# A fused adaLN, linear attention and GEGLU kernel: first-LN transposes by DMA, den and broadcasts by pairs of token groups, woven among Q blocks and KV*wo

## The chip, the cores, the metric

One NeuronCore of one Trainium2 chip. The metric is the device time of one execution in microseconds, and smaller is better. A quoted time is the median of a kernel's runs in the fast state. A profile describes one of those executions; its span is about 1.8 us shorter than that execution's time (899.0 us beside 900.79 for the kernel before).

Engines, as the profile names them: PE is TensorE (PEld its weight loads), DVE is VectorE, ACT is ScalarE, POOL is GpSimd, SP is SyncE, which issues most DMAs. In the traces each engine takes its instructions in the order of the program: VectorE's scaling at 287.46 us below, for instance, stands behind two modulations that it does not need. The granted clock is the share of full speed that TensorE's clock was given, as the profile records it; a stretch near 0.5 is called cold.

## The reference, cut to what matters

```python
# x: 2048 tokens x 1024, bf16; 32 heads of 32; F = 3584
h = _layernorm(x) * (1 + ca) + sa             # first LN, modulated by a row per feature
q, k, v = split(h @ wqkv)
phi = lambda t: where(t > 0, t + 1, exp(t)) + 1e-6
kv = einsum('bhsd,bhse->bhde', phi(k), v)     # over ALL tokens
z  = einsum('bhsd->bhd', phi(k))
den = einsum('bhqd,bhd->bhq', phi(q), z) + 1e-6
x = x + ga * ((phi(q) @ kv / den) @ wo)
h = _layernorm(x) * (1 + cb) + sb             # second LN
x = x + gb * ((gelu(h @ w_gate) * (h @ w_up)) @ w_down)
```

kv and z need every token before the first output of the attention can be made. So the program has a first pass over 16 chunks of 128 tokens (LN, K, V, accumulation of kv, and Q of earlier token groups beside it), then an end of that pass with the last Q group and den, then the output product, then the FFN over four groups of 512 tokens.

## The kernel before

`T, A, V, G, Q` are TensorE, ScalarE, VectorE, GpSimd and SyncE. `sch.op` appends an instruction to an engine's list and works out its waits from the bytes that it reads and writes, so the order of these Python lines is the order of each engine's work. Cuts are marked `# ...`.

```python
def t1(c_, tb):            # transpose chunk c_ of the normalised x into h1T
    for dc in range(NDC):
        sch.op(T, lambda e, dc=dc: e.transpose(PS16(tb, dc * P, (dc + 1) * P), b_[:, dc * P:(dc + 1) * P], IDENT[:, :]), ...)
    sch.op(A, lambda e: e.activation(H1[sg][:, :, ci * P:(ci + 1) * P], PS16(tb)..., ACTF.Copy), ...)

def phi(bank, dst_ap, dst_rng, note):      # exponential, min/add, addition
    sch.op(A, ... e.activation(EB[i], PS(bank), ACTF.Exp) ...)
    sch.op(V, ... e.tensor_scalar(EB[i], EB[i], 1.0, 1e-6, op0=ALU.min, op1=ALU.add) ...)
    sch.op(V, ... e.scalar_tensor_tensor(dst_ap, PS(bank), 0.0, EB[i], op0=ALU.max, op1=ALU.add) ...)

for c_ in range(4, NCH):                        # THE LOOP
    # ...
    if c_ + 2 < NCH:
        t1(c_ + 2, 4)                           # PSUM bank 4
        if c_ % 2 == 1:
            mod1(c_ + 1, 2)                     # x(1+ca)+sa of two chunks, on VectorE
    for _ in range(2):
        q_block(*q_todo.pop(0))
    # ... two K blocks, two V blocks, each with its eviction
    kvacc(c_ - 1)
    if c_ + 3 < NCH:
        ln1(c_ + 3)                             # statistics and normalisation of chunk c_+3, on VectorE
    # ... at 6 and 9: modulation rows through bank 4; at 10: selector matrices on GpSimd

q_block(3, 0)                                   # THE LAST Q GROUP
kvacc(NCH - 1)
q_block(3, 1)
zcols()
kvbd()
q_block(3, 2)
den(0)                                          # 32 matmuls 128 wide, reciprocal, split in two bf16
kvt()
q_block(3, 3)
for g in range(NG):
    w2_pair(g)                                  # KV*wo: two matmuls, a copy of 128x1024 by ScalarE
    if g % 2 == 1:
        q_block(3, 4 + g // 2)
    if g == 3:
        den(1)
den(2)
# ... bcast(0, 0..1): spread 1/den over the features in PSUM; pq_scale: multiply phi(q) by it

for sg in range(3):                             # THE WO STAGE, chunks 0 to 11
    for ci in range(CPG):
        c_ = sg * CPG + ci
        wo_chunk(c_, 4 + 2 * (ci % 2))          # 16 matmuls, then x1 = PSUM + x on VectorE
        if ci < 2:
            bcast(sg + 1, ci)
            for j in range(CPG):
                pq_scale(sg + 1, ci, j)
        if c_ == 2:
            den(3)
        if sg == 1:
            ln2_a(ci, False)                    # second LN of chunk ci, its DMA transpose
            if ci == 3:
                mod2(0, 2)
    if sg == 1:
        mod2(2, 2)                              # waits for the transposes of chunks 2 and 3
# ... FFN; wo chunks 12 to 15 stand in it
```

Of the kernel before, what the change touches and what calls it, by code (L numbers as in the profile page):

```python
# [10 lines left out]
P = 128  # L11
# [205 lines left out]
def bass_adaLN_cond__linear_attn_block__geglu_ffn__prompt_kernel(  # L217
# [14 lines left out]
    with ExitStack() as es:  # L232
# [30 lines left out]
        RDHL = at("rdhl", [P, NSG, 2, P], bf16, OFF_RDHL)  # L263
# [24 lines left out]
        for name, shape, dty, sz in [  # L288
            ("ident", [P, P], bf16, 256), ("bmask", [P, P], bf16, 256), ("bm32", [P, NG, NH], bf16, 512),
            ("z32", [P, NG, NH], bf16, 512), ("rd0", [P, P], f32, 512), ("rd1", [P, P], f32, 512),  # L290
# [14 lines left out]
        RDC = [_small["rd0"], _small["rd1"]]  # L305
# [48 lines left out]
        def r_rdhl(sg, k):  # L354
            return [(OFF_RDHL + (sg * 2 + k) * 256, OFF_RDHL + (sg * 2 + k + 1) * 256, "rdhl")]
# [157 lines left out]

        def mods(Ht, rfn, sg, scT, biT, sn, bn, s0, s1, dc0=0, dc1=NDC, tag=""):
# [48 lines left out]
        def phi(bank, dst_ap, dst_rng, note):  # L563
# [4 lines left out]
            sch.op(V, lambda e: e.tensor_scalar(EB[i][:, :], EB[i][:, :], 1.0, 1e-6, op0=ALU.min, op1=ALU.add),  # L568
                   rd=rng, wr=rng, note=f"{note}.min")
# [45 lines left out]
        def q_block(sg, qc):  # L615
            b = nb()
# [7 lines left out]
            phi(b, PQ[sg][:, qc, :], r_pq(sg, qc, qc + 1), f"phiq{sg}.{qc}")  # L624
# [32 lines left out]
        for c_ in range(4):  # L657
            for jg in range(2):
                b = nb()
                kv_mm(c_, "v", jg, b, list(range(NDC)))  # L660
                v_evac(c_, jg, b)
            if c_ == 0:
                ln1(4)
                for k, t in enumerate((4, 5, 10, 11)):
                    wm_dma(t, k)
            if c_ >= 1:
                kvacc(c_ - 1)
            if c_ == 1:
                ln1(5)
            if c_ == 2:  # L670
                t1(4, 4)
                mod1(4, 1)
                ln1(6)
                x_dma(12, 16)
        t1(5, 4)
        mod1(5, 1)
# [3 lines left out]
        for c_ in range(4, NCH):  # L680
            if c_ % 4 == 0:
                q_todo += [(c_ // 4 - 1, qc) for qc in range(NG)]
            if c_ + 2 < NCH:
                t1(c_ + 2, 4)
                if c_ % 2 == 1:
                    mod1(c_ + 1, 2)
# [6 lines left out]
            for jg in range(2):  # L693
                b = nb()
                kv_mm(c_, "v", jg, b, list(range(NDC)))
                v_evac(c_, jg, b)
            kvacc(c_ - 1)
            if c_ + 3 < NCH:
                ln1(c_ + 3)
            if c_ == 6:  # L700
# [16 lines left out]
            if c_ == 10:  # L717
# [37 lines left out]
        def w2_pair(g):  # L755
            b0 = 4 + 2 * (g % 2)
# [7 lines left out]
        def den(sg):  # L764
            b = nb()
            o = None
            for g in range(NG):
                for j in range(CPG):
                    o = sch.op(T, lambda e, g=g, j=j: e.matmul(ps_all[32 * j:32 * (j + 1), b * 512:b * 512 + P], Z32[:, g, :],
                                                               PQ[sg][:, g, j * P:(j + 1) * P], start=(g == 0), stop=(g == NG - 1)),  # L770
                               rd=r_sm("z32") + r_pq(sg, g, g + 1, j * P, (j + 1) * P), pwr=(pr(b) if g == 0 else ()), note=f"den{sg} {g}.{j}")
            pset_writer(b, o)
            k = sg % 2
            rn = f"rd{k}"
            sch.op(V, lambda e: e.tensor_scalar(RDC[k][:, :], PS(b, 0, P), 1e-6, None, op0=ALU.add), prd=pr(b), wr=r_sm(rn), note=f"dene{sg}")
            sch.op(V, lambda e: e.reciprocal(RDC[k][:, :], RDC[k][:, :]), rd=r_sm(rn), wr=r_sm(rn), note=f"rden{sg}")
            sch.op(G, lambda e: e.tensor_copy(RDHL[:, sg, 0, :], RDC[k][:, :]), rd=r_sm(rn), wr=r_rdhl(sg, 0), note=f"rdhi{sg}")
            sch.op(G, lambda e: e.tensor_tensor(RDHL[:, sg, 1, :], RDC[k][:, :], RDHL[:, sg, 0, :], ALU.subtract),
                   rd=r_sm(rn) + r_rdhl(sg, 0), wr=r_rdhl(sg, 1), note=f"rdlo{sg}")

        def bcast(sg, gh):
            o = [None] * 4
            for g in range(4 * gh, 4 * gh + 4):
                for k in range(2):
                    for j in range(CPG):
                        b = j
                        o[j] = sch.op(T, lambda e, g=g, k=k, j=j, b=b: e.matmul(  # L787
                            PS(b, (g % 4) * P, (g % 4 + 1) * P), SEL[32 * j:32 * (j + 1), g, :], RDHL[32 * j:32 * (j + 1), sg, k, :],
                            start=(k == 0), stop=(k == 1)),
                            rd=R_SEL + r_rdhl(sg, k), pwr=(pr(b) if g % 4 == 0 and k == 0 else ()), note=f"bc{sg} {g}.{k}.{j}")  # L790
            for j in range(CPG):
                pset_writer(j, o[j])

        def pq_scale(sg, gh, j):
            ap = PQ[sg][:, 4 * gh:4 * gh + 4, j * P:(j + 1) * P]
            rng = r_pq(sg, 4 * gh, 4 * gh + 4, j * P, (j + 1) * P)
            sch.op(V, lambda e: e.tensor_tensor(ap, ap, PS(j).rearrange("p (a b) -> p a b", a=4), ALU.mult),
                   prd=pr(j), rd=rng, wr=rng, note=f"pqs{sg}.{gh}.{j}")

        q_block(3, 0)  # L800
        kvacc(NCH - 1)
        q_block(3, 1)
        zcols()
        kvbd()
        q_block(3, 2)
        den(0)
        kvt()
        q_block(3, 3)
        for g in range(NG):
            w2_pair(g)  # L810
            if g % 2 == 1:
                q_block(3, 4 + g // 2)
            if g == 3:
                den(1)
        den(2)
# [221 lines left out]
```

## Time and profile before

| | before |
|---|---|
| time, median of the first 3 runs (of 4 with the forecast's rounds) | 899.84 us (900.04) |
| span of the profiled run | 899.0 us |
| TensorE, first V block to first Q block | 40.62 to 58.95: 18.3 us |
| the loop, chunks 4 to 15 | 58.95 to 210.53: 151.6 us |
| last Q group, den, KV*wo, first broadcasts | 210.53 to 238.16: 27.6 us |
| wo stage, chunks 0 to 11 | 238.16 to 299.49: 61.3 us |
| FFN | 299.49 to the end: 599.5 us |

The stages are read from the timeline of TensorE, from the first matmul of one kind to the first of the next. Single matmul records can be missing from a trace, so an edge can be off by some 0.2 us.

Three lines of the page of the kernel before: busy time (us, share of the span, number of instructions), then TensorE's busy tenths and its granted clock in 40 slices of 22.5 us.

```profile
PE 852.5 (95%) x4569; PEld 394.2 (44%) x4569; DVE 503.4 (56%) x912; ACT 300.6 (33%) x481; POOL 36.2 (4%) x65
...
PE   3999998899895999999999999999999999999998
...
PEclk9999999999898999999999999999999999999999
```

TensorE is 95% busy. That does not say that nothing can be gained: the busy time of the page counts a matmul at a lower clock as fully busy (between 292 and 296 us below: 4.00 of 4.00 us busy at a clock of 0.71). The timeline says more. Its columns: start, duration, engine, line, operation, operands, number of instructions merged into the row, and in brackets the idle time before it and what ended it.

```profile
58.95 3.62 PE L619 MATMUL ps_all<-h1T_50,wq 128*128 128x512 bf16 x16
62.41 3.62 PE L578 MATMUL ps_all<-wk,h1T_51 128*128 128x512 bf16 x16
65.86 3.62 PE L578 MATMUL ps_all<-wv,h1T_51 128*128 128x512 bf16 x16
69.31 0.62 PE L600 MATMUL ps_all<-vs_78,pk_76 128*128 128x129 bf16 x8
70.93 0.62 PE L509 MATMUL ps_all<-ident,xh_105 128*128 128x128 bf16 x8 [1.00 <-DVE xh_105 L484]
71.39 3.62 PE L619 MATMUL ps_all<-h1T_50,wq 128*128 128x512 bf16 x16
```

Sixteen 128x512 matmuls take 3.45 us from start to start, 0.216 us each. One iteration needs 10.82 us of them: Q, K, V at 3.45 each and 0.45 for the accumulation (`vs,pk`). But the row at 70.93, the eight transposes of one chunk (`ident,xh`), is late by 1.00 us: it waited for VectorE's normalised chunk (`xh`). Such a wait, of 0.87 to 2.38 us, stands before the transposes of all iterations that have them (in two, 0.87 us each, it ends with ScalarE's copy of a modulation row). The longest such wait is this:

```profile
160.52 0.62 PE L600 MATMUL ps_all<-vs_79,pk_73 128*128 128x129 bf16 x8
163.51 0.62 PE L509 MATMUL ps_all<-ident,xh_106 128*128 128x128 bf16 x8 [2.38 <-DVE xh_106 L484]
163.97 5.30 PE L619 MATMUL ps_all<-h1T_52,wq 128*128 128x512 bf16 x16
```

After the wait of 2.38 us, sixteen Q matmuls take 5.14 us from start to start (163.97 to 169.11) instead of 3.45: the granted clock is 0.57 between 164 and 168.

The wo stage has the greatest loss. Rows 277.66 and 290.95 are output products (`w,pq`), those between them broadcasts (`rdhl,sel`):

```profile
277.66 3.63 PE L834 MATMUL ps_all<-w_65,pq_56 128*128 128x512 bf16 x16
288.19 0.28 PE L787 MATMUL ps_all<-rdhl,sel 32*128 32x128 bf16 x1 [6.91 <-DVE pq_57 L797]
288.79 0.28 PE L787 MATMUL ps_all<-rdhl,sel 32*128 32x128 bf16 x1 [0.32 <-DVE pq_57 L797]
...
290.95 8.71 PE L834 MATMUL ps_all<-w_65,pq_56 128*128 128x512 bf16 x32
```

TensorE stood for 6.91 us before one broadcast. It waited for VectorE's scaling L797. The same stretch on VectorE:

```profile
279.74 2.14 DVE L516 TENSOR_SCALAR h2T_58<-h2T_58,cb1T,sbT 128x256 bf16<-128x256 bf16 x8
284.27 2.14 DVE L516 TENSOR_SCALAR h2T_58<-h2T_58,cb1T,sbT 128x256 bf16<-128x256 bf16 x8 [2.39 <-DMA h2T_58<-xh_104]
286.33 1.22 DVE L841 TENSOR_TENSOR xall<-ps_all,xall 128x1024 bf16<-128x1024 f32 x1
287.46 2.47 DVE L797 TENSOR_TENSOR pq_57<-pq_57,ps_all 128x512 bf16<-128x512 bf16 x4
```

The row at 284.27, a second-LN modulation (L516), waited 2.39 us for a DMA transpose. The x1 additions (L841) and the scalings (L797), which TensorE needs, stand behind both modulations in VectorE's order although they do not depend on them. And windows of 4 us show what TensorE's standing costs afterwards (columns: window, length, busy time of the engines, the granted clock `PEclk`, DMA share, GB/s):

```profile
284.00:288.00 4.00, 0.00 (x0) 0.00 (x0) 3.73 (x10) 0.00 (x0) 0.00 (x0) 0.51 0.00 0
288.00:292.00 4.00, 2.86 (x35) 1.49 (x36) 4.00 (x7) 0.00 (x0) 0.00 (x0) 0.50 0.00 0
292.00:296.00 4.00, 4.00 (x14) 1.51 (x13) 1.46 (x3) 0.00 (x0) 0.00 (x0) 0.71 0.96 259
```

The granted clock is 0.51 and 0.50 in the first two of these windows and 0.71 in the third, and 32 matmuls from 291.01 on took 8.64 us in the chain of waits and not 6.91.

### The profile page before, as it was taken

To read this page: it belongs to the slowest core of one execution; us is meant where nothing else is said; L and a number is where in the kernel's file an instruction comes from. 1 tells how busy PE (TensorE), PEld (TensorE's weight loads), DVE (VectorE), ACT (ScalarE), POOL (GpSimd) and SP (SyncE) were. 2 spreads that over 40 slices of the span, in tenths; PEclk is the share of its full clock that TensorE was granted. 3 is DMA by queue.
4 is the path that set the end of the run, shared out by engine and by line. 5 is a ranking of instruction groups with operands and counts; after the bars stand their busy time and mean duration, and the time that the engine had idled before them with its cause. 6 is when DMAs were issued, how large, how long until landed. Compare 5 with 4: busy or idle time off the path is not lost.

```text
span 899.0 us, 11946 instructions
## 1 busy us (share of the span) xinstructions
PE 852.5 (95%) x4569; PEld 394.2 (44%) x4569; DVE 503.4 (56%) x912; ACT 300.6 (33%) x481; POOL 36.2 (4%) x65
## 2 busy tenths in 40 slices
PE   3999998899895999999999999999999999999998
PEld 2444444444342444444444444444444444444443
DVE  5476565666677455556436566535565643565512
ACT  4243333334201233453025454204545302545300
POOL 2000004200000000000000000000000000000000
PEclk9999999999898999999999999999999999999999
DMA  9940603000602345834135553306553413565000
GB/s 321 360 162 1 208 28 95 1 1 24 211 9 41 95 116 166 279 96 127 47 106 144 165 160 94 71 24 172 156 141 101 122 47 105 150 168 152 1 24 23
DMA packets 165096, 101.46 MB, mean 113 GB/s; under 512 B 21928, under 2 KB 157096, under 8 KB 165040
## 3 DMA queue, kind: packets, MB, share of 16 engines
q1 hardware_dynamic: 165040, 100.70, 38.9%
q8 instruction: 36, 0.59, 0.3%
q14 instruction: 20, 0.16, 0.1%
HBM read 92.28 MB, written 4.21 MB: 107 GB/s over the span
## 4 chain that ended last, share of the span: by engine, by line
PE 89%; DVE 6%; issue 2%; POOL 1%; ACT 1%; DMA 1%; SPq 0%; ACTq 0%; POOLq 0%; DVEq 0%
PE ps_all L897 22%; PE ps_all L921 22%; PE ps_all L894 21%; PE ps_all L578 10%; PE ps_all L619 6%; PE ps_all L834 5%; POOL rs L475 1%; DVE st L471 1%; PE ps_all L509 1%; DVE st L470 1%; PE ps_all L550 0%; PE ps_all L600 0%; PE ps_all L787 0%; PE ps_all L534 0%; PE ps_all L759 0%
## 5 line engine op out<-in xcount | busy, mean ns | idle before, releaser
L905 ACT ACTIVATE q_0_109<-ps_all 128x512 f32<-128x512 f32 x56 | 33.5, 598 | 183.3 <-PE ps_all L894 183.3
L927 DVE TENSOR_TENSOR ps_all<-ps_all,gbb 128x512 f32<-128x512 f32 x32 | 22.4, 698 | 95.7 <-PE ps_all L921 95.7
L907 DVE SCALAR_TENSOR_TENSOR ww_111<-q_0_109,ps_all 128x512 f32<-128x512 f32 x56 | 38.5, 687 | 56.9 <-ACT guh_96 L906 56.9
L910 DVE SCALAR_TENSOR_TENSOR ww_111<-th_113,guh_96 128x512 f32<-128x512 f32 x56 | 38.8, 693 | 39.0 <-ACT th_113 L909 39.0
L910 DVE SCALAR_TENSOR_TENSOR ww_112<-th_114,guh_97 128x512 f32<-128x512 f32 x56 | 38.8, 692 | 39.0 <-ACT th_114 L909 39.0
L907 DVE SCALAR_TENSOR_TENSOR ww_112<-q_1_110,ps_all 128x512 f32<-128x512 f32 x56 | 38.5, 687 | 37.1 <-ACT guh_97 L906 37.1
L905 ACT ACTIVATE q_1_110<-ps_all 128x512 f32<-128x512 f32 x56 | 33.5, 597 | 55.4 <-PE ps_all L894 54.2
L909 ACT ACTIVATE th_114<-ww_112 128x512 f32<-128x512 f32 x56 | 35.3, 630 | 42.2 <-DVE ww_112 L907 42.2
L909 ACT ACTIVATE th_113<-ww_111 128x512 f32<-128x512 f32 x56 | 35.3, 630 | 42.2 <-DVE ww_111 L907 42.2
L475 POOL TENSOR_TENSOR rs<-ve,neghalf 128x1 f32<-128x1 f32 x32 | 17.6, 551 | 606.3 <-DVE ve L473 592.7
L912 DVE TENSOR_TENSOR yT<-ww_111,ps_all 128x512 bf16<-128x512 f32 x56 | 38.4, 687 | 1.9
L912 DVE TENSOR_TENSOR yT<-ww_112,ps_all 128x512 bf16<-128x512 f32 x56 | 38.4, 687 | 1.9
L906 ACT ACTIVATE guh_96<-ps_all 128x512 f32<-128x512 f32 x56 | 33.1, 592 | 0.0
L906 ACT ACTIVATE guh_97<-ps_all 128x512 f32<-128x512 f32 x56 | 33.1, 592 | 0.0
L921 PE MATMUL ps_all<-wd_66,yT 128*128 128x512 bf16 x128 | 32.9, 379 | 0.0
L921 PE MATMUL ps_all<-wd_69,yT 128*128 128x512 bf16 x128 | 32.9, 379 | 0.0
L921 PE MATMUL ps_all<-wd_72,yT 128*128 128x512 bf16 x128 | 32.9, 379 | 0.0
L921 PE MATMUL ps_all<-wd_67,yT 128*128 128x512 bf16 x128 | 32.9, 379 | 0.0
L921 PE MATMUL ps_all<-wd_68,yT 128*128 128x512 bf16 x128 | 32.9, 379 | 0.0
L921 PE MATMUL ps_all<-wd_70,yT 128*128 128x512 bf16 x128 | 32.9, 379 | 0.0
L921 PE MATMUL ps_all<-wd_71,yT 128*128 128x512 bf16 x128 | 32.9, 379 | 0.0
L897 PE MATMUL ps_all<-h2T_60,wu_93 128*128 128x512 bf16 x80 | 30.3, 379 | 1.4 <-DVE xall L929 1.4
(291 smaller groups left out, 1731.0 us busy)
## 6 DMA issues: line engine op xcount, KB each, us to landing
wg_90<-in_B_w_gate_dram SPq DMA_DIRECT2D x20, 512.0 KB, 3.8
wu_93<-in_B_w_up_dram SPq DMA_DIRECT2D x20, 512.0 KB, 5.1
wg_91<-in_B_w_gate_dram SPq DMA_DIRECT2D x20, 512.0 KB, 4.1
wu_94<-in_B_w_up_dram SPq DMA_DIRECT2D x20, 512.0 KB, 5.1
wg_92<-in_B_w_gate_dram SPq DMA_DIRECT2D x16, 512.0 KB, 3.9
wu_95<-in_B_w_up_dram SPq DMA_DIRECT2D x16, 512.0 KB, 5.1
out_dram<-xall SPq DMA_DIRECT2D x32, 128.0 KB, 1.7
wmst_81<-in_w_mod_dram SPq DMA_DIRECT2D x3, 1024.0 KB, 7.5
```

The lines of the kernel that those rows point to most:

```text
L578: o = sch.op(T, lambda e, dc=dc: e.matmul(PS(bank), H1[sg][:, dc, ci * P:(ci + 1) * P], W_[:, dc, jg * 512:(jg + 1) * 512], start=(dc == 0 ...
L619: o = sch.op(T, lambda e, dc=dc: e.matmul(PS(b), WQ[:, dc, qc * P:(qc + 1) * P], H1[sg][:, dc, :], start=(dc == 0), stop=(dc == NDC - 1)), ...
L834: last[half] = sch.op(T, lambda e, g=g, half=half: e.matmul(PS(b0 + half), PQ[sg][:, g, ci * P:(ci + 1) * P], W2[:, g, half * 512:(half + ...
L894: og = sch.op(T, lambda e, dc=dc: e.matmul(PS(bg), WG[slot][:, dc, e_ * P:(e_ + 1) * P], H2[sg][:, dc, :], start=(dc == 0), stop=(dc == ND ...
L897: ou = sch.op(T, lambda e, dc=dc: e.matmul(PS(bu), WU[slot][:, dc, e_ * P:(e_ + 1) * P], H2[sg][:, dc, :], start=(dc == 0), stop=(dc == ND ...
L905: sch.op(A, lambda e: e.activation(Q1[j][:, :], PS(bg), ACTF.Square, scale=math.sqrt(GELU_A)), prd=pr(bg), wr=rq, note=f"q1 {fc}")
L906: ogh = sch.op(A, lambda e: e.activation(GUH[j][:, :], PS(bg), ACTF.Copy, scale=0.5), prd=pr(bg), wr=rg, note=f"gh {fc}")
L907: sch.op(V, lambda e: e.scalar_tensor_tensor(WW[j][:, :], Q1[j][:, :], 1.0, PS(bg), op0=ALU.add, op1=ALU.mult), rd=rq, prd=pr(bg), wr=rw, ...
L909: sch.op(A, lambda e: e.activation(TH[j][:, :], WW[j][:, :], ACTF.Tanh, scale=GELU_C), rd=rw, wr=rt, note=f"th {fc}")
L910: sch.op(V, lambda e: e.scalar_tensor_tensor(WW[j][:, :], TH[j][:, :], 1.0, GUH[j][:, :], op0=ALU.add, op1=ALU.mult), rd=rt + rg, wr=rw, n ...
L912: sch.op(V, lambda e: e.tensor_tensor(YT[:, fc, :], WW[j][:, :], PS(bu), ALU.mult), rd=rw, prd=pr(bu), wr=r_yt(fc), note=f"yT {fc}")
L921: o = sch.op(T, lambda e, b=b, fc=fc, half=half: e.matmul(PS(b), YT[:, fc, ci * P:(ci + 1) * P], WDT[fc // 4][:, fc % 4, half * 512:(half ...
```

## The change

Its intent: take the transposes of tokens 512 on off TensorE and their copies off ScalarE; make den and its broadcast in half as many, twice as wide matmuls; spread the broadcasts of the first pair among the last Q blocks and KV*wo. With it some lines move: modulation after the V blocks, selector matrices after iteration 13 and not 10, the second LN one chunk later, second-LN modulations after chunks 9 and 10, and the min/add of four Q blocks goes to GpSimd.

```diff
+        def tdma(stream, dst, src, rng, wr_, note):
+            d_ = [last_t[0]] if last_t[0] is not None and last_t[0].stream != stream else []
+            last_t[0] = sch.dma(stream, lambda e: e.dma_start_transpose(out=dst, in_=src), rd=rng, wr=wr_, deps=d_, note=note)
 ...
-        def phi(bank, dst_ap, dst_rng, note):
+        def phi(bank, dst_ap, dst_rng, note, min_eng=V):
 ...     # min/add on min_eng; q_evac: G if sg == NSG - 1 and qc >= 4 else V
             if c_ == 0:
                 ln1(4)
+                t1d(4, A)
 ...
             if c_ == 1:
                 ln1(5)
+                t1d(5, A)
             if c_ == 2:
-                t1(4, 4)
-                mod1(4, 1)
                 ln1(6)
                 x_dma(12, 16)
-        t1(5, 4)
-        mod1(5, 1)
+                t1d(6)
+        mod1(4, 2)
 ...     # in the loop
-            if c_ + 2 < NCH:
-                t1(c_ + 2, 4)
-                if c_ % 2 == 1:
-                    mod1(c_ + 1, 2)
 ...     # Q, K, V blocks
+            if c_ % 2 == 1 and c_ + 2 < NCH:
+                mod1(c_ + 1, 2)
             kvacc(c_ - 1)
             if c_ + 3 < NCH:
                 ln1(c_ + 3)
+                t1d(c_ + 3)
 ...
-            if c_ == 10:
+            if c_ == 13:     # selector matrices on GpSimd
 ...
         def w2_pair(g):
-            b0 = 4 + 2 * (g % 2)
+            b0 = 2
 ...     # den(pair): 32 matmuls 256 wide; bcast(pair, r): 16 matmuls 256 wide and four scalings
-        q_block(3, 0) ... den(0) ... w2_pair(g), q_block, den(1), den(2)
+        q_block(3, 0, False, 0)
+        kvacc(NCH - 1)
+        zcols()
+        q_evac(3, 0, 0)
+        q_block(3, 1, bank=1)
+        kvbd()
+        q_block(3, 2, bank=2)
+        den(0, 5)
+        kvt()
+        q_block(3, 3, bank=0)
+        w2_pair(0)
+        q_block(3, 4, bank=1)
+        bcast(0, 0)
+        w2_pair(1)
+        q_block(3, 5, bank=0)
+        w2_pair(2)
+        bcast(0, 1)
+        w2_pair(3)
+ ...     # and so on to bcast(0, 3), w2_pair(7)
-        for sg in range(3): ...
+        for c_ in range(12):
+            wo_chunk(c_, 2 * (c_ % 2))
+            if c_ == 1:
+                den(1, 4)
+            if 3 <= c_ < 7:
+                bcast(1, c_ - 3)
+            if 5 <= c_ < 9:
+                ln2_a(c_ - 5, False)
+            if c_ == 9:
+                mod2(0, 2)
+            if c_ == 10:
+                mod2(2, 2)
```

`tdma` lets a transpose issued from one engine's queue wait for the last one issued from another's.

More of the change, by code (lines that the diff above doesn't have):

```diff
@@ L262, in bass_adaLN_cond__linear_attn_block__geglu_ffn__prompt_kernel @@
         SEL = at("sel", [P, NG, P], bf16, OFF_SEL)
-        RDHL = at("rdhl", [P, NSG, 2, P], bf16, OFF_RDHL)
+        RDHL = at("rdhl", [P, 2, 2, SGW // 2], bf16, OFF_RDHL)
         IOTA_B = at("iota_b", [P, NG * P], i32, OFF_IOTA2)
@@ L289, in bass_adaLN_cond__linear_attn_block__geglu_ffn__prompt_kernel @@
             ("ident", [P, P], bf16, 256), ("bmask", [P, P], bf16, 256), ("bm32", [P, NG, NH], bf16, 512),
-            ("z32", [P, NG, NH], bf16, 512), ("rd0", [P, P], f32, 512), ("rd1", [P, P], f32, 512),
+            ("z32", [P, NG, NH], bf16, 512), ("rdc", [P, SGW // 2], f32, 1024),
             ("silr", [P, NDC, 32], bf16, 512),
@@ L304, in bass_adaLN_cond__linear_attn_block__geglu_ffn__prompt_kernel @@
         IDENT, BMASK, BM32, Z32 = _small["ident"], _small["bmask"], _small["bm32"], _small["z32"]
-        RDC = [_small["rd0"], _small["rd1"]]
+        RDC = _small["rdc"]
         SILR, C8, CT, CHALF, THC, SILUT = (_small[k] for k in ("silr", "c8", "cT", "chalf", "thc", "siluT"))
@@ L354, in r_rdhl @@
         def r_rdhl(sg, k):
-            return [(OFF_RDHL + (sg * 2 + k) * 256, OFF_RDHL + (sg * 2 + k + 1) * 256, "rdhl")]
+            return [(OFF_RDHL + (sg * 2 + k) * 512, OFF_RDHL + (sg * 2 + k + 1) * 512, "rdhl")]
         R_SEL = [(OFF_SEL, OFF_SEL + 2048, "sel")]
@@ L512, in t1, with t1d @@
                    prd=pr(tb), wr=r_h1(sg, 0, NDC, ci * P, (ci + 1) * P), note=f"h1raw {c_}")
+        last_t = [None]
+        def tdma(stream, dst, src, rng, wr_, note):
+            d_ = [last_t[0]] if last_t[0] is not None and last_t[0].stream != stream else []
+            last_t[0] = sch.dma(stream, lambda e: e.dma_start_transpose(out=dst, in_=src), rd=rng, wr=wr_, deps=d_, note=note)
+        def t1d(c_, stream=Q):
+            b_, rng = xh_buf(c_)
+            sg, ci = divmod(c_, CPG)
+            tdma(stream, H1[sg][:, :, ci * P:(ci + 1) * P], b_[:, :], rng, r_h1(sg, 0, NDC, ci * P, (ci + 1) * P), f"T1 {c_}")
         def mods(Ht, rfn, sg, scT, biT, sn, bn, s0, s1, dc0=0, dc1=NDC, tag=""):
@@ L567, in phi @@
             sch.op(A, lambda e: e.activation(EB[i][:, :], PS(bank), ACTF.Exp), prd=pr(bank), wr=rng, note=f"{note}.exp")
-            sch.op(V, lambda e: e.tensor_scalar(EB[i][:, :], EB[i][:, :], 1.0, 1e-6, op0=ALU.min, op1=ALU.add),
-                   rd=rng, wr=rng, note=f"{note}.min")
+            o = sch.op(min_eng, lambda e: e.tensor_scalar(EB[i][:, :], EB[i][:, :], 1.0, 1e-6, op0=ALU.min, op1=ALU.add),
+                       rd=rng, wr=rng, deps=[last_g[0]] if min_eng == G else [], note=f"{note}.min")
+            if min_eng == G:
+                last_g[0] = o
             sch.op(V, lambda e: e.scalar_tensor_tensor(dst_ap, PS(bank), 0.0, EB[i][:, :], op0=ALU.max, op1=ALU.add),
@@ L613, in nb, with q_block @@
             return b
-        def q_block(sg, qc):
-            b = nb()
+        def q_block(sg, qc, evac=True, bank=None):
+            b = nb() if bank is None else bank
             o = None
@@ L623, in q_block, with q_evac @@
             pset_writer(b, o)
-            phi(b, PQ[sg][:, qc, :], r_pq(sg, qc, qc + 1), f"phiq{sg}.{qc}")
+            if evac:
+                q_evac(sg, qc, b)
+            return b
+        def q_evac(sg, qc, b):
+            phi(b, PQ[sg][:, qc, :], r_pq(sg, qc, qc + 1), f"phiq{sg}.{qc}", G if sg == NSG - 1 and qc >= 4 else V)
         for c_ in range(3):
@@ L762, in w2_pair, with den @@
                    prd=pr(b0) + pr(b0 + 1), wr=r_w(OFF_WK, "w2", g), note=f"w2cp{g}")
-        def den(sg):
-            b = nb()
+        HW = SGW // 2
+        def den(pr_, b):
             o = None
             for g in range(NG):
-                for j in range(CPG):
-                    o = sch.op(T, lambda e, g=g, j=j: e.matmul(ps_all[32 * j:32 * (j + 1), b * 512:b * 512 + P], Z32[:, g, :],
-                                                               PQ[sg][:, g, j * P:(j + 1) * P], start=(g == 0), stop=(g == NG - 1)),
-                               rd=r_sm("z32") + r_pq(sg, g, g + 1, j * P, (j + 1) * P), pwr=(pr(b) if g == 0 else ()), note=f"den{sg} {g}.{j}")
-            pset_writer(b, o)
-            k = sg % 2
-            rn = f"rd{k}"
-            sch.op(V, lambda e: e.tensor_scalar(RDC[k][:, :], PS(b, 0, P), 1e-6, None, op0=ALU.add), prd=pr(b), wr=r_sm(rn), note=f"dene{sg}")
-            sch.op(V, lambda e: e.reciprocal(RDC[k][:, :], RDC[k][:, :]), rd=r_sm(rn), wr=r_sm(rn), note=f"rden{sg}")
-            sch.op(G, lambda e: e.tensor_copy(RDHL[:, sg, 0, :], RDC[k][:, :]), rd=r_sm(rn), wr=r_rdhl(sg, 0), note=f"rdhi{sg}")
-            sch.op(G, lambda e: e.tensor_tensor(RDHL[:, sg, 1, :], RDC[k][:, :], RDHL[:, sg, 0, :], ALU.subtract),
-                   rd=r_sm(rn) + r_rdhl(sg, 0), wr=r_rdhl(sg, 1), note=f"rdlo{sg}")
@@ L781, in bcast @@
-        def bcast(sg, gh):
+                for i in range(4):
+                    sg, t0 = 2 * pr_ + i // 2, (i % 2) * HW
+                    o = sch.op(T, lambda e, g=g, i=i, sg=sg, t0=t0: e.matmul(
+                        ps_all[32 * i:32 * (i + 1), b * 512:b * 512 + HW], Z32[:, g, :], PQ[sg][:, g, t0:t0 + HW],
+                        start=(g == 0), stop=(g == NG - 1)),
+                        rd=r_sm("z32") + r_pq(sg, g, g + 1, t0, t0 + HW), pwr=(pr(b) if g == 0 else ()), note=f"den{pr_} {g}.{i}")
@@ new lines, in den @@
+            pset_writer(b, o)
+            sch.op(V, lambda e: e.tensor_scalar(RDC[:, :], PS(b, 0, HW), 1e-6, None, op0=ALU.add), prd=pr(b), wr=r_sm("rdc"), note=f"dene{pr_}")
+            sch.op(V, lambda e: e.reciprocal(RDC[:, :], RDC[:, :]), rd=r_sm("rdc"), wr=r_sm("rdc"), note=f"rden{pr_}")
+            o = sch.op(G, lambda e: e.tensor_copy(RDHL[:, pr_, 0, :], RDC[:, :]), rd=r_sm("rdc"), wr=r_rdhl(pr_, 0), deps=[last_g[0]], note=f"rdhi{pr_}")
+            last_g[0] = sch.op(G, lambda e: e.tensor_tensor(RDHL[:, pr_, 1, :], RDC[:, :], RDHL[:, pr_, 0, :], ALU.subtract),
+                   rd=r_sm("rdc") + r_rdhl(pr_, 0), deps=[o], wr=r_rdhl(pr_, 1), note=f"rdlo{pr_}")
@@ L782, in bcast @@
+        def bcast(pr_, r):
             o = [None] * 4
-            for g in range(4 * gh, 4 * gh + 4):
+            for gi in range(2):
                 for k in range(2):
-                    for j in range(CPG):
-                        b = j
-                        o[j] = sch.op(T, lambda e, g=g, k=k, j=j, b=b: e.matmul(
-                            PS(b, (g % 4) * P, (g % 4 + 1) * P), SEL[32 * j:32 * (j + 1), g, :], RDHL[32 * j:32 * (j + 1), sg, k, :],
+                    for i in range(4):
+                        o[i] = sch.op(T, lambda e, gi=gi, k=k, i=i: e.matmul(
+                            PS(4 + i, gi * HW, (gi + 1) * HW), SEL[32 * i:32 * (i + 1), 2 * r + gi, :], RDHL[32 * i:32 * (i + 1), pr_, k, :],
@@ L789, in bcast @@
                             start=(k == 0), stop=(k == 1)),
-                            rd=R_SEL + r_rdhl(sg, k), pwr=(pr(b) if g % 4 == 0 and k == 0 else ()), note=f"bc{sg} {g}.{k}.{j}")
-            for j in range(CPG):
-                pset_writer(j, o[j])
-        def pq_scale(sg, gh, j):
-            ap = PQ[sg][:, 4 * gh:4 * gh + 4, j * P:(j + 1) * P]
-            rng = r_pq(sg, 4 * gh, 4 * gh + 4, j * P, (j + 1) * P)
-            sch.op(V, lambda e: e.tensor_tensor(ap, ap, PS(j).rearrange("p (a b) -> p a b", a=4), ALU.mult),
-                   prd=pr(j), rd=rng, wr=rng, note=f"pqs{sg}.{gh}.{j}")
@@ L800, in bass_adaLN_cond__linear_attn_block__geglu_ffn__prompt_kernel, with pq_scale @@
-        q_block(3, 0)
+                            rd=R_SEL + r_rdhl(pr_, k), pwr=(pr(4 + i) if gi == 0 and k == 0 else ()), note=f"bc{pr_} {r}.{gi}.{k}.{i}")
+            for i in range(4):
+                pset_writer(4 + i, o[i])
+            for i in range(4):
+                pq_scale(pr_, r, i)
+        def pq_scale(pr_, r, i):
+            sg, t0 = 2 * pr_ + i // 2, (i % 2) * HW
+            ap = PQ[sg][:, 2 * r:2 * r + 2, t0:t0 + HW]
+            rng = r_pq(sg, 2 * r, 2 * r + 2, t0, t0 + HW)
+            sch.op(V, lambda e: e.tensor_tensor(ap, ap, PS(4 + i).rearrange("p (a b) -> p a b", a=2), ALU.mult),
+                   prd=pr(4 + i), rd=rng, wr=rng, note=f"pqs{pr_}.{r}.{i}")
@@ L801, in bass_adaLN_cond__linear_attn_block__geglu_ffn__prompt_kernel @@
+        q_block(3, 0, False, 0)
         kvacc(NCH - 1)
-        q_block(3, 1)
         zcols()
+        q_evac(3, 0, 0)
+        q_block(3, 1, bank=1)
         kvbd()
-        q_block(3, 2)
-        den(0)
+        q_block(3, 2, bank=2)
+        den(0, 5)
         kvt()
-        q_block(3, 3)
-        for g in range(NG):
-            w2_pair(g)
-            if g % 2 == 1:
-                q_block(3, 4 + g // 2)
-            if g == 3:
-                den(1)
-        den(2)
+        q_block(3, 3, bank=0)
@@ L817, in bass_adaLN_cond__linear_attn_block__geglu_ffn__prompt_kernel @@
+        w2_pair(0)
[6 more added lines that the diff above has]
+        w2_pair(3)
+        q_block(3, 6, bank=1)
+        w2_pair(4)
+        bcast(0, 2)
+        w2_pair(5)
+        q_block(3, 7, bank=0)
+        w2_pair(6)
+        bcast(0, 3)
+        w2_pair(7)
         wd_q = [0]
@@ L853, in ln2_a @@
             sg, ci = divmod(c_, CPG)
-            sch.dma(Q, lambda e: e.dma_start_transpose(out=H2[sg][:, :, ci * P:(ci + 1) * P], in_=b_[:, :]),
-                    rd=rng, wr=r_h2(sg, 0, NDC, ci * P, (ci + 1) * P), note=f"T2 {c_}")
+            tdma(Q, H2[sg][:, :, ci * P:(ci + 1) * P], b_[:, :], rng, r_h2(sg, 0, NDC, ci * P, (ci + 1) * P), f"T2 {c_}")
         stream_pair(0, 0)
@@ L860, in bass_adaLN_cond__linear_attn_block__geglu_ffn__prompt_kernel @@
             wd_dma(q)
-        for gh in range(2):
-            bcast(0, gh)
-            for j in range(CPG):
-                pq_scale(0, gh, j)
-        for sg in range(3):
-            for ci in range(CPG):
-                c_ = sg * CPG + ci
-                wo_chunk(c_, 4 + 2 * (ci % 2))
-                if ci < 2:
-                    bcast(sg + 1, ci)
-                    for j in range(CPG):
-                        pq_scale(sg + 1, ci, j)
-                if c_ == 2:
-                    den(3)
-                if sg == 1:
-                    ln2_a(ci, False)
-                    if ci == 3:
-                        mod2(0, 2)
-            if sg == 1:
+        for c_ in range(12):
[9 more added lines that the diff above has]
+            if c_ == 10:
                 mod2(2, 2)
```

## The prediction

> **What bounds it now.** TensorE: on the page it is busy for 95% of the 899.0 us span and 89% of the chain that ended last. The timeline shows 128x512 matmuls at a pitch of 0.216 us (16 in 3.45). The FFN starts at 299.5 us and hardly has a gap; the diff leaves it alone. Before it, the timeline shows:
> - chunks 4 to 15, from the first Q block at 58.95 to 210.5: 151.6 us. Twelve times 10.82 (Q, K, V, KV accumulation) and two modulation groups of 1.95 make 133.7. The rest: nine transpose groups (0.45 each), waits before them (0.87 to 2.38, 10.9 together) and a cold stretch (16 matmuls in 5.14; granted clock 0.57).
> - last Q group, den, KV*wo, first broadcasts: 27.7 us; from 232.2 it mostly waits for VectorE (reciprocal, scaling).
> - wo chunks 0 to 11, 238.2 to 299.5: 61.3 us for 41.5 of matmuls. Waits: 1.85 (x1 eviction); 6.9 and 3 x 0.32 before a broadcast, with VectorE held in order by a second-LN transpose. Near clock 0.5, 5.97 and 8.64 us for what takes 3.45 and 6.91.
>
> [...]after the 6.9 us wait it is 0.50 here[...].
>
> **What the change does.**
> 1. Transposes leave TensorE, and their 1.02 us copies ScalarE. A DMA transpose lands in 3.1 us here and takes its issuer 1.24, one per 10.8 us, with over 4 us of slack before its modulation. VectorE has 8 to 9.6 us of work per 10.8, so the loop should run at matmul pitch: 134 to 136 us (gain 16.5). Ahead of it, ScalarE waits in order for chunks 4 and 5 and holds V evictions up: 1 us lost against 3.0 of transposes and waits removed; first Q block near 57 (gain 2).
> 2. den and broadcasts by pairs: half the matmuls, twice as wide; 1 to 2 us.
> 3. Broadcasts woven in. KV*wo has one bank pair, so the second of two neighbours waits some 0.7 us for the 1.02 us copy; four scalings of 0.6 hold the next broadcast up. By hand I get 25 us for 27.7 (gain 3).
> 4. wo stage: 41.5 + 0.9 (den) + 1.8 (broadcasts). VectorE has about 41 us of work there and falls behind in chunks 5 to 8 (x1 1.2, scaling 2.4, LN 2.6 against 3.9 of TensorE). I expect 2.3 us of wait at chunk 9 and 2 before the FFN (second half of the second modulation): 49 us for 61.3 (gain 12 to 13), without cold stretches.
>
> Sum: the FFN starts near 265, and the end comes 34 us earlier: **866 us**, range 858 to 876. Faster by over 2%: 0.94; within 2%: 0.05; slower: 0.01.
>
> **What shows it right.** Timeline: first Q block near 57, loop 134 to 136 us without 1 us gaps, first wo chunk near 215, FFN near 265 and as long as before. Windows: clock 1.00 through the loop and most of wo; VectorE over 90% busy in the wo stage. Waits: TensorE none for a normalised chunk, some for KV*wo copies, scaling, x1.
>
> **What would make it wrong.** First two DMA transposes (50 to 57 us) much later than 3.1 us beside weight loads; GpSimd's min/add for four Q blocks (not in this trace; I assume 1 to 1.5 us) slowing the scaling; waits in wo growing until the clock falls; VectorE slowed by GpSimd's selector building.

Two clauses around "after the 6.9 us wait it is 0.50 here" are cut from this text; "it" there is the granted clock. The sum: gains of 2, 16.5, 3 and 12 to 13 us come to 34 (the 1 to 2 us of the pairs are not added apart), and 900 less 34 is 866.

## The result

870.29 us (868.06 to 870.71, 4 runs) against 900.04 us (898.96 to 900.86, 4 runs): ratio 0.9665, 95% interval 0.9645 to 0.9685, faster. A ratio here compares the fast runs of the same rounds by their means, so it is not quite the ratio of the medians quoted beside it. The forecast of 866 us, range 858 to 876, held.

| stage, us | before | after | forecast |
|---|---|---|---|
| first V block to first Q block | 18.3 | 16.6 | 16 to 17 (2 less) |
| loop | 151.6 | 134.2 | 134 to 136 |
| last Q group, den, KV*wo | 27.6 | **28.4** | **25** |
| wo stage | 61.3 | 48.2 | 49 |
| FFN | 599.5 | 599.7 | the same |
| FFN starts at | 299.5 | 266.6 | 265 |

The page of the kernel after, the same lines:

```profile
PE 832.9 (96%) x4201; PEld 384.2 (44%) x4281; DVE 500.1 (58%) x896; ACT 288.1 (33%) x469; POOL 43.2 (5%) x65
...
PE   3999999998989999999999999999999999999998
...
PEclk9999999999999999999999999999999999999999
```

The loop, on TensorE, beside the first fence of before: there is no transpose in it and no row waits for `xh`.

```profile
55.82 3.62 PE L632 MATMUL ps_all<-h1T_50,wq 128*128 128x512 bf16 x16
59.27 3.88 PE L591 MATMUL ps_all<-wk,h1T_51 128*128 128x512 bf16 x15
62.99 3.62 PE L591 MATMUL ps_all<-wv,h1T_51 128*128 128x512 bf16 x16
66.44 0.62 PE L613 MATMUL ps_all<-vs_78,pk_76 128*128 128x129 bf16 x8
66.90 3.62 PE L632 MATMUL ps_all<-h1T_50,wq 128*128 128x512 bf16 x16
```

An iteration takes 66.90 - 55.82 = 11.08 us here and 10.82 in the later ones without modulation rows, which is the 10.82 us of matmuls alone. The 0.27 us more are in the first K block (59.27 to 62.99, 3.72 us and not 3.45): its weight loads wait for VectorE's first modulation piece by piece, eight times, 1.4 us in all.

The wo stage keeps one wait of some size, 1.95 us before chunk 9, and 0.24 before the FFN:

```profile
249.73 3.62 PE L864 MATMUL ps_all<-w_65,pq_56 128*128 128x512 bf16 x15
255.30 11.06 PE L864 MATMUL ps_all<-w_65,pq_56 128*128 128x512 bf16 x47 [1.95 <-DVE xall L871]
266.60 0.38 PE L915 MATMUL ps_all<-h2T_58,wg_90 128*128 128x512 bf16 x1 [0.24 <-DVE h2T_58 L527]
```

On VectorE, just before, the x1 addition (L871) that frees the bank stands behind the scaling (L817) and the second LN (L470 and following), as the forecast had worked out:

```profile
250.24 1.27 DVE L817 TENSOR_TENSOR pq_57<-pq_57,ps_all 128x512 bf16<-128x512 bf16 x2
251.43 0.68 DVE L470 BATCH_NORM_STATS2 st<-xall 128x6 f32<-128x512 bf16 x1
...
254.02 1.22 DVE L871 TENSOR_TENSOR xall<-ps_all,xall 128x1024 bf16<-128x1024 f32 x1
```

The last Q group became longer, not shorter. TensorE, from the sixth Q block on:

```profile
202.66 1.89 PE L632 MATMUL ps_all<-h1T_53,wq 128*128 128x512 bf16 x8
204.38 0.59 PE L776 MATMUL ps_all<-wo,kvt 128*128 128x512 bf16 x2
206.18 0.28 PE L804 MATMUL ps_all<-rdhl,sel 32*128 32x256 bf16 x1 [1.20 <-DVE pq_54 L817]
206.78 0.28 PE L804 MATMUL ps_all<-rdhl,sel 32*128 32x256 bf16 x1 [0.32 <-DVE pq_54 L817]
...
207.97 0.61 PE L804 MATMUL ps_all<-rdhl,sel 32*128 32x256 bf16 x13 [0.32 <-DVE pq_55 L817]
```

It waits 1.20 + 3 x 0.32 us for the scaling of the broadcast before. VectorE and GpSimd then:

```profile
201.00 0.69 DVE L583 SCALAR_TENSOR_TENSOR pq_57<-ps_all,eb_103 128x512 bf16<-128x512 f32 x1
204.84 0.69 DVE L583 SCALAR_TENSOR_TENSOR pq_57<-ps_all,eb_98 128x512 bf16<-128x512 f32 x1 [3.14 <-POOL eb_98 L579]
205.45 1.27 DVE L817 TENSOR_TENSOR pq_54<-pq_54,ps_all 128x512 bf16<-128x512 bf16 x2
```

```profile
202.87 1.94 POOL L579 TENSOR_SCALAR eb_98<-eb_98 128x512 f32<-128x512 f32 x1 [1.37 <-ACT eb_98 L578]
```

GpSimd's min/add takes 1.94 us, where VectorE's in the same kernel mostly takes 0.41 to 0.43 (up to 1.25 while GpSimd works beside it). VectorE stands idle for 3.14 us until it is done, because the addition (L583) at 204.84 must come before the scaling in its order. So the 1.94 us are not a matter of the two engines working at once, and VectorE goes on 0.03 us after their end.

One more thing is in the list of runs. The profiled run of the kernel after is its fastest (868.06 us, mean granted clock 0.998). The other three took 869.87 to 870.71 at a clock of 0.995 or 0.996. The forecast had no such term.

### The profile page after: what moved, and what is told of

Same layout as the page of the kernel before. It is cut to its first block, busy times and chain, and to the rows that moved or that the text cites. A ratio compares the mean times of both kernels' runs of the same rounds, so it can differ in the third digit from the quotient of the medians.

```text
span 866.3 us, 11297 instructions
## 1 busy us (share of the span) xinstructions
PE 832.9 (96%) x4201; PEld 384.2 (44%) x4281; DVE 500.1 (58%) x896; ACT 288.1 (33%) x469; POOL 43.2 (5%) x65
## 4 chain that ended last, share of the span: by engine, by line
PE 88%; DVE 6%; issue 2%; POOL 1%; ACT 1%; DMA 1%; ACTq 0%; SPq 0%; POOLq 0%; DVEq 0%
PE ps_all L918 23%; PE ps_all L942 22%; PE ps_all L915 21%; PE ps_all L591 10%; PE ps_all L632 6%; PE ps_all L864 4%; DVE st L471 1%; DVE st L470 1%; POOL rs L475 1%; PE ps_all L613 1%; DVE xall L871 1%; PE ps_all L561 0%; PE ps_all L545 0%; DMA h2T_58<-xh_104 0%; DMA xall<-in_A_x_dram 0%
## 5 line engine op out<-in xcount | busy, mean ns | idle before, releaser
L926 ACT ACTIVATE q_0_109<-ps_all 128x512 f32<-128x512 f32 x56 | 33.4, 597 | 169.2 <-PE ps_all L915 161.5
L926 ACT ACTIVATE q_1_110<-ps_all 128x512 f32<-128x512 f32 x56 | 33.4, 597 | 54.9 <-PE ps_all L915 52.9
L942 PE MATMUL ps_all<-wd_66,yT 128*128 128x512 bf16 x128 | 32.9, 379 | 0.0
L942 PE MATMUL ps_all<-wd_70,yT 128*128 128x512 bf16 x128 | 32.8, 379 | 0.0
L942 PE MATMUL ps_all<-wd_72,yT 128*128 128x512 bf16 x124 | 32.6, 379 | 0.2
L942 PE MATMUL ps_all<-wd_69,yT 128*128 128x512 bf16 x124 | 32.6, 379 | 0.2
L942 PE MATMUL ps_all<-wd_68,yT 128*128 128x512 bf16 x125 | 32.4, 379 | 0.2
L942 PE MATMUL ps_all<-wd_67,yT 128*128 128x512 bf16 x125 | 32.2, 379 | 0.2
L942 PE MATMUL ps_all<-wd_71,yT 128*128 128x512 bf16 x124 | 32.0, 379 | 0.2
```

The lines of the kernel that those rows point to most:

```text
L926: sch.op(A, lambda e: e.activation(Q1[j][:, :], PS(bg), ACTF.Square, scale=math.sqrt(GELU_A)), prd=pr(bg), wr=rq, note=f"q1 {fc}")
L942: o = sch.op(T, lambda e, b=b, fc=fc, half=half: e.matmul(PS(b), YT[:, fc, ci * P:(ci + 1) * P], WDT[fc // 4][:, fc % 4, half * 512:(half ...
```

## The experiments

All outputs are right. Stages are read as above. The kernel before, run in the same rounds, took 899.0 to 899.6 us in the median (single runs 895.7 to 901.1), and 900.04 in the rounds of the kernel after. So two labels of different rounds compare in time only to about 1 us; the ratios are safer.

| label | us | ratio to before (95%) | V to Q | loop | last Q group | wo stage |
|---|---|---|---|---|---|---|
| (after) | 870.29 | 0.9665 (0.9645 to 0.9685) | 16.6 | 134.2 | 28.4 | 48.2 |
| t1_only | 880.79 | 0.9796 (0.9769 to 0.9824) | slow profile | | | |
| t1_only_b | 879.84 | 0.9787 (0.9756 to 0.9818) | 16.1 | 133.9 | 27.8 | 60.4 |
| weave_only | 887.90 | 0.9872 (0.9846 to 0.9897) | 18.3 | 149.4 | 28.3 | 48.2 |
| pe_late | 871.78 | 0.9705 (0.9676 to 0.9734) | 16.1 | 138.1 | 30.0 | 48.2 |
| min_v | 865.52 | 0.9628 (0.9602 to 0.9654) | 16.1 | 133.7 | 25.5 | 48.2 |
| min_g8 | 874.16 | 0.9723 (0.9697 to 0.9749) | 16.1 | 133.9 | 33.4 | 48.2 |
| wo_order | 866.97 | 0.9640 (0.9615 to 0.9664) | 16.1 | 133.9 | 30.1 | 52.1 (14 chunks) |
| combo | 862.34 | 0.9589 (0.9565 to 0.9613) | 16.1 | 133.9 | 25.3 | 52.1 (14 chunks) |
| iota | 897.69 | 0.9977 (0.9964 to 0.9991) | 18.3 | 149.6 | 27.8 | 59.9 |
| mod2_late | 893.64 | 0.9934 (0.9921 to 0.9946) | 18.3 | 150.1 | 27.8 | 53.2 |
| moves_only | 876.12 | 0.9740 (0.9727 to 0.9753) | 16.1 | 138.3 | 27.8 | 51.5 |
| t1_sp | 879.98 | 0.9784 (0.9771 to 0.9797) | 15.2 | 144.4 | 29.8 | 48.2 |

### Do the two halves add? t1_only, t1_only_b, weave_only

t1_only and t1_only_b are one kernel: before, with only the transposes moved.

```diff
             if c_ == 0:
                 ln1(4)
+                t1d(4, A)
 ...     # the first-LN lines of the change, and nothing else of it
```

> The kernel before with only the transposes of tokens 512 on moved to DMA. Theory (the waits before the transposes go, not only their array time): first Q block about 2 us earlier, loop of chunks 4 to 15 in 134 to 137 us instead of 151.6, last Q group and wo stage as before (27.7 and about 61 us), so about 881 us (878 to 885). Rival (the DMA saves only the 4.5 us of array time, the waits turn up elsewhere, for instance as later modulations): about 894 us.

> The same kernel as t1_only once more, since its profile fell in a slow execution and shows no stages. First Q block about 16.5 us after the first V block (18.3 before), loop 134 to 137 us, last Q group about 27.7, wo stage 60 to 61 us; about 881 us. Rival: loop over 145 us with new waits for modulated chunks.

The first of them had one slow execution, which was the profiled one: 1283.47 us at a mean granted clock of 0.658. It came once, no run shows why, and it is left out of the ratio and of everything below. The second profile is of a fast run: loop 133.9 us, last Q group 27.8, wo stage 60.4. The rival (only the array time is saved) falls.

weave_only is the opposite: after, with `t1` and its `mod1` lines as before.

```diff
-                t1d(c_ + 3)
+            if c_ + 2 < NCH:                    # at the head of the iteration
+                t1(c_ + 2, 4)
+                if c_ % 2 == 1:
+                    mod1(c_ + 1, 2)
```

> The changed kernel with the transposes put back on TensorE as they were. Theory (the two halves add): loop about 149 us (the selector build now comes after the last normalisation, so the 2.4 us wait and its cold stretch go), last Q group 28.4, wo stage 48 us, so about 886 us (883 to 889). Rival (the wo stage gains only because the loop hands over earlier): wo stage over 55 us, 893 us or more.

Loop 149.4, wo stage 48.2. So the wo stage gains by itself and not from an earlier hand-over. The shares saved are 1 - 0.9787 = 2.1% and 1 - 0.9872 = 1.3%, together 3.4%; the whole change has 1 - 0.9665 = 3.35%. The halves add.

### Was it the DMA, or the waits? pe_late

```diff
             for _ in range(2):
                 q_block(*q_todo.pop(0))
+            if c_ + 2 < NCH:
+                t1(c_ + 2, 4)                   # TensorE again, 3.45 us later in the iteration
 ...
             if c_ + 3 < NCH:
                 ln1(c_ + 3)
-                t1d(c_ + 3)
```

> The changed kernel with the transposes on TensorE again, but each placed after the two Q blocks of its iteration instead of before them, 3.5 us later, when its normalised chunk should be ready. Theory (the loop gained 17 us mostly from waits, and only about 4 us from array time): loop about 138.5 us, first Q block as late as before, total about 876 us (874 to 879). Rival (transposes on TensorE cost the waits wherever they stand, so that only DMA removes them): loop 148 us or more, 884 us or more.

The loop takes 138.1 us, and in it no transpose waits; in one iteration, for instance, they start 3.45 us after the start of the two Q blocks, which is what these need:

```profile
68.71 3.62 PE L632 MATMUL ps_all<-h1T,wq 128*128 128x512 bf16 x16
72.16 0.61 PE L509 MATMUL ps_all<-ident,xh 128*128 128x128 bf16 x8
```

Of the 17.4 us that the loop gained in the change, the moved lines give 13.5 (the transposes by two Q blocks within their iteration, and the selector matrices, see iota below); the DMA gives the other 3.9, near the 4.5 that the ten groups of transposes in this loop need on TensorE at 0.45 us each. (The first Q block came early too, 16.1 us after the first V block, although chunks 4 and 5 were as before: the third transpose moved behind the first two Q blocks.) The total was 871.78 us, below the expected 874 to 879, and only 1.5 us above the kernel after. The list of runs shows why: three of its five runs were at a clock of 0.998, three of the four of the kernel after at less. At 0.998 alone it is 871.5 to 871.8 against 868.06, and the difference of 3.5 to 3.7 us is that of the loops. Its profiled run was one of the slower two (875.05 us, clock 0.996) and shows where the time goes. Windows of 2 us in the last Q group:

```profile
212.00:214.00 2.00, 1.06 (x14) 0.58 (x15) 2.00 (x4) 0.00 (x0) 1.11 (x1) 0.91 0.01 2
214.00:216.00 2.00, 2.00 (x12) 0.58 (x5) 1.78 (x4) 0.52 (x1) 0.00 (x0) 0.50 0.00 0
216.00:218.00 2.00, 2.00 (x8) 0.84 (x7) 0.73 (x2) 0.51 (x1) 0.00 (x0) 0.74 0.60 171
```

After waits of 0.93 + 3 x 0.32 us before a broadcast, the clock is 0.50 for part of a Q block, which took 2.66 us from start to start (215.18 to 217.84) and not 1.73. wo_order, with the same instructions in this stage, shows the same in its profile: 0.50 between 210 and 212, 30.1 us for the stage. The same stage took 28.4 us in the profile of the kernel after, at a clock of 1.00 throughout, although its waits (1.20 + 3 x 0.32) are those of wo_order. So after such waits the clock came down in some executions and not in others. weave_only has the same four waits as pe_late, and the Q block after them took 1.73 us from start to start (226.31 to 228.04). It is the same with the wait of 2.38 us in the loop: in the kernel before it is followed by a clock of 0.57, while in mod2_late the fifteen recorded Q matmuls after it took 3.24 us from start to start (164.57 to 167.81), 0.216 each. That the slower runs of the kernel after have the cold stretch too is inferred from their lower mean clock; they left no trace.

### The mis-sized term: min_v, min_g8

```diff
-            phi(b, PQ[sg][:, qc, :], r_pq(sg, qc, qc + 1), f"phiq{sg}.{qc}", G if sg == NSG - 1 and qc >= 4 else V)
+            phi(b, PQ[sg][:, qc, :], r_pq(sg, qc, qc + 1), f"phiq{sg}.{qc}", V)                               # min_v
+            phi(b, PQ[sg][:, qc, :], r_pq(sg, qc, qc + 1), f"phiq{sg}.{qc}", G if sg == NSG - 1 else V)       # min_g8
```

> The changed kernel with the min/add of the last four Q blocks on VectorE again instead of GpSimd (1.93 us each there, VectorE waits 3.1, 2.65 and 0.92 us for them). Theory (this is the term my forecast mis-sized: 25 us forecast, 28.4 measured for the last Q group): 25 to 26.5 us for the stage, total 2 to 3 us below the changed kernel, about 867.5. Rival (the single bank pair of KV*wo and the four scalings set the pace of the stage, so the min's engine does not matter): stage 28 us or more, 870 us.

> The changed kernel with the min/add of all eight last Q blocks on GpSimd, instead of four. Theory (1.93 us on GpSimd against 0.43 on VectorE lengthens the stage through the order of VectorE's work): last Q group 30 to 32 us instead of 28.4 (25.5 with none), and where the clock falls 1 to 2.5 us more; total 872 to 875 us. Rival (only the blocks beside broadcasts matter): 28.4 us, 870 us.

With none, four and eight of the min/adds on GpSimd the stage takes 25.5, 28.4 (30.0 and 30.1 where the clock fell) and 33.4 us. So min_v comes to the 25 us that the forecast had for the change. What the stage takes with the 1 to 1.5 us that the forecast assumed for GpSimd was not run. min_v's VectorE in the same place:

```profile
203.33 0.43 DVE L579 TENSOR_SCALAR eb<-eb 128x512 f32<-128x512 f32 x1 [1.04 <-ACT eb L578]
203.79 0.69 DVE L583 SCALAR_TENSOR_TENSOR pq<-ps_all,eb 128x512 bf16<-128x512 f32 x1
204.39 2.47 DVE L817 TENSOR_TENSOR pq<-pq,ps_all 128x512 bf16<-128x512 bf16 x4
```

The min (L579) takes 0.43 us and the scaling (L817) follows at once. min_v's four runs lie between 865.01 and 865.88 us, all at a clock of 0.998. No wait before a broadcast is longer than 0.32 us there, and the clock fell in none of them. The median of 865.52 was lower than the expected 867.5: it is 2.5 us below the kernel after at the same clock (868.06), as expected, and 4.8 below its median, in which the lower clock counts too. In min_g8, whose stage was longer than expected (30 to 32), the clock falls twice, to 0.50 in windows at 202 and at 216 us; its total of 874.16 us was within the expected 872 to 875.

### The wait in the wo stage: wo_order, combo

```diff
-        for c_ in range(12):
+        for c_ in range(14):
             wo_chunk(c_, 2 * (c_ % 2))
 ...
-            if 5 <= c_ < 9:
-                ln2_a(c_ - 5, False)
-            if c_ == 9:
+            if 7 <= c_ < 11:
+                ln2_a(c_ - 7, False)
+            if c_ == 11:
                 mod2(0, 2)
-            if c_ == 10:
+            if c_ == 12:
                 mod2(2, 2)
```

(and wo chunks 12 and 13 leave the FFN). combo has this and min_v's line.

> The changed kernel with the second LN of the first four chunks two wo chunks later (7 to 10), its modulations at 11 and 12, and wo chunks 12 and 13 before the FFN instead of in it. Theory (VectorE has over 6 us of work per 3.9 us chunk at chunks 5 and 6, and so TensorE waits 1.95 us at chunk 9 and 0.24 before the FFN): these two waits go, about 2.2 us less than the changed kernel, 868 us (866 where the clock does not fall in the last Q group). Rival (the stage is bound by VectorE's sum of work, so the waits only move): no difference, 870 us.

> min_v and wo_order together. If the two causes are separate stages, their gains add: about 4.8 us and 2.2 us below the changed kernel, 863 us (862 to 864), ratio 0.960 to the kernel before. If min_v moved the load of VectorE into the wo stage, the gain of wo_order shrinks: 865 us.

In wo_order the waits of 1.95 and 0.24 us are gone. Its stage now holds two more chunks of 3.45 us, so its 52.1 us compare with 48.2 + 6.9 = 55.1; the FFN is 7.0 us shorter (592.7). That is 3.0 us of gain and somewhat more than the two waits (2.2); where the rest comes from was not looked into. Its total was 866.97 us, with all four runs at the lower clock, where 868 had been expected. combo: 862.34 us against an expected 863, ratio 0.9589; the two gains add (865.52 and 866.97 each alone). It beats both kernels and is the version to keep.

### How much of the change was the order of lines? iota, mod2_late, moves_only

All three are the kernel before with lines moved.

```diff
-            if c_ == 10:                        # iota: selector matrices
+            if c_ == 13:
```

> The kernel before with GpSimd's selector building after iteration 13 instead of 10 (and the wait that the check then needs before GpSimd's next instruction). Theory (the selectors delay the normalisations of chunks 13 and 14, which costs a wait of 1.76 and one of 2.38 us and a cold stretch of 1.7): loop about 149 us instead of 151.6, total 897 us (896 to 898.5). Rival (noise): 899.5.

897.69 us, as expected, and the interval excludes no change. The wait of 2.38 us is gone; the one of 1.76 stays, at a later chunk, which the theory had not expected. One of 0.71 us came, before a V block (182.87): TensorE waits there for VectorE's addition (L570); why that comes late the views of this run do not show. How its 2 us divide among the stages stays open: the same loop took 151.6 us in one profile of unmoved lines and 150.1 in another.

```diff
                 if sg == 1:                     # mod2_late
                     ln2_a(ci, False)
-                    if ci == 3:
-                        mod2(0, 2)
-            if sg == 1:
-                mod2(2, 2)
+                if c_ == 9:
+                    mod2(0, 2)
+                    mod2(2, 2)
```

> The kernel before with both second-LN modulations of the first four chunks moved from before wo chunk 8 to after chunk 9 and its scaling. Theory (most of the wo stage's gain comes from VectorE no longer standing in order behind a DMA transpose before a scaling, not from pairing): wait before the broadcast at chunk 9 falls from 6.9 to 2 or 3 us, no cold stretch after it, wo stage 52.5 to 55 us instead of 61.3, total about 891.5 us (889 to 894). Rival (pairing den and broadcasts is what gains): wo stage over 59 us, 898 us or more.

The broadcast that had waited 6.91 us waits 0.28, less than the expected 2 or 3, and three others beside it 0.37 or 0.38 each:

```profile
279.60 0.22 PE L787 MATMUL ps_all<-rdhl,sel 32*128 32x128 bf16 x1 [0.28 <-DVE pq L797]
```

The wo stage takes 53.2 us in place of 61.3. The unmoved stage took 59.9 and 60.4 us in the profiles of iota and t1_only_b. So of the 13.1 us that the change gains there, two modulations that no longer stand before scalings in VectorE's order give 7 to 8 by themselves. In time it gained less, 0.66% or 5.9 us: the profiled run was its fastest (891.78), the others took 1.5 to 2.5 us more at a lower mean clock, and no trace shows where.

moves_only has these two, and the transposes on TensorE after the Q blocks, and the modulation after the V blocks.

> The kernel before with moved lines alone: transposes stay on TensorE but stand after the two Q blocks, modulation after the V blocks, selectors after iteration 13, second-LN modulations after chunk 9. No DMA transpose in the first LN, no pairs, no weaving. Theory (the change's gain was mostly waits that the order of the lines made): loop 138 us, last Q group 27.7, wo stage 52.5 to 55, total 876 to 880 us, so over two thirds of the change's gain of 29.8 us. Rival (DMA transposes and pairing are needed): 888 us or more.

876.12 us, ratio 0.9740. No DMA transpose in the first LN, no pairs, no weaving, and 2.60 of the change's 3.35%, more than three quarters of its gain. pe_late, which has the moves, the pairs and the weaving but TensorE's transposes, has 2.95%. So in this order pairs and weaving add about 0.35% and the DMA transposes 0.4%, each only just clear of intervals that reach 0.13 to 0.3% to either side.

### The issuer of the first transposes: t1_sp

```diff
-                t1d(4, A)
+                t1d(4)                          # from SyncE
 ...
-                t1d(5, A)
+                t1d(5)
```

> The changed kernel with the first two DMA transposes issued from SyncE instead of ScalarE. Their 9.3 and 7.1 us to landing came beside weight loads. In SyncE's own queue they stand behind 2 MB of loads; ScalarE is no longer held, so the 0.43 us wait of TensorE for a V eviction goes. Theory (behind the loads they land later, and the modulation of chunk 4 comes after TensorE needs it): a new wait of 1 to 3 us at the first K block of chunk 4, total 871 to 873. Rival ([...]the issuer makes no difference): total 869.5 to 870.3.

879.98 us, 9.7 us above the kernel after (1.2% by the ratios), when 1 to 3 had been expected by the one theory and nothing by the other. SyncE's issues (SPq) and, below, VectorE's first modulation:

```profile
50.11 1.36 SPq L518 DMA_TRANSPOSE h1T<-xh  x1
51.58 5.73 SPq L433 DMA_DIRECT2D wmst<-in_w_mod_dram  x4
57.41 5.83 SPq L518 DMA_TRANSPOSE h1T<-xh  x1
```

```profile
66.84 2.14 DVE L527 TENSOR_SCALAR h1T<-h1T,ca1T,saT 128x256 bf16<-128x256 bf16 x8 [10.88 <-DMA h1T<-xh]
```

Both theories missed the larger part. SyncE is in order as well: it stands until 50.11, when chunk 4 is normalised, and the four 1 MB loads that follow in its list, which the kernel after issues between 33.9 and 45.5, go out from 51.58 on. The transpose of chunk 5 then stands behind 4 MB. VectorE waits 10.88 us for it, TensorE 7.77 us before the first K block of chunk 4, and the clock is 0.50 until after 72 us. In the kernel after, where ScalarE issues these two, they land 9.3 and 7.1 us after issue, beside the same loads; VectorE waits 4.3 us for them, and TensorE loses only the 0.27 us of its first K block.

## Why the prediction was right, point by point

- *"TensorE bounds it, only the stretch before the FFN can change"*: right. The FFN took 599.5 and 599.7 us.
- *Loop at matmul pitch, 134 to 136 us*: right, 134.2. pe_late shows that the reason given, waits more than array time, holds: 138.1 us with the transposes still on TensorE.
- *First Q block near 57, ScalarE holding V evictions*: right, with some luck in the place: it came at 55.8 in a run that reached the first V block 1.4 us earlier (39.26), before anything that the change touches; in the profiles of the twelve other runs with stages that block comes at 39.7 to 42.7. From V block to Q block it took 16.6 us, where the forecast amounts to 16.4. The held V eviction made TensorE wait 0.43 us and not 1. The forecast's risk, late first transposes, came true (9.3 and 7.1 us) and used up the slack: the modulation came with the first K block, which took 0.27 us longer.
- *"Broadcasts woven in ... By hand I get 25 us for 27.7 (gain 3)"*: this is the term that was wrong. It measured 28.4 us in the profiled run, a loss of 0.8 where 3 had been booked as a gain. GpSimd's min/add of a 128x512 tile takes 1.9 us; the forecast assumed 1 to 1.5 although nothing in the trace of before measured it, and named it as a risk. It lies in the chain from exponential to addition to scaling to the next broadcast. min_v, without it, takes 25.5 us. That the assumed 1 to 1.5 us would have given 25 stays open.
- *The clock*: the forecast held cold stretches for gone. In the profiled run they are; in three of four runs the mean clock is 0.995 or 0.996 and the time 1.8 to 2.7 us longer. pe_late and wo_order show a place for the same instructions: the last Q group, after waits that the min/adds on GpSimd lengthen (0.93 and 1.20 us before a broadcast, where min_v has none over 0.32). For the kernel after itself it is inferred. With min_v's line all runs are at 0.998.
- *wo stage 49 us with 2.3 us at chunk 9 and 2 before the FFN*: total right (48.2), the first wait right in place and size (1.95), the second only 0.24. "VectorE over 90% busy" was wrong: 36.9 us busy of 48.2, 76%. VectorE was late in a few chunks, not full; wo_order could therefore remove the waits by moving work.
- *"VectorE slowed by GpSimd's selector building"*: this risk came true without harm. Beside it, four min/adds of VectorE took 0.53 to 1.25 us (162 to 168 us); TensorE's timeline shows no wait of 0.3 us or more there.
- *Sum*: 866 forecast, 868.06 in the profiled run, 870.29 in the median. In the profiled run the last Q group is 3.4 us over its forecast, and the first Q block, the loop and the wo stage are each about 1 us under theirs, so the sum is nearer than its worst term. The other runs, at a lower clock, are 1.8 to 2.7 us longer.

What the forecast did not ask is which part of the change was needed. moves_only and combo answer it: most of the gain was the order of lines, of TensorE's transposes and of VectorE's modulations above all, and the change's own move of four instructions to GpSimd gave some of it back.

## What to carry to other kernels

When the busiest engine has waits of 1 us in every iteration, ask first whether the instruction that waits could stand a few microseconds later in the same engine's list, and whether what it waits for stands behind something unrelated in another engine's list; here such moves gave 23 of 30 us with no new mechanism. Before an instruction goes to an idle engine, measure it there (here 1.94 us on GpSimd for 0.41 to 0.43 on VectorE), and look whether it lies in a chain that the bound engine waits for. A DMA that must wait for its data held the later DMAs of the same issuing engine (in t1_sp four loads of 1 MB went out from 51.58 us on, which the kernel after issued from 33.9 on), so issue such a one from an engine whose later work can afford the wait, and look at what stands behind it.
